# Retention attention feeding a gated MLP, one core: key casts of the first two units on ScalarE, and a new fixed order of all engines

## The chip, the cores and the metric

The kernel runs on one core of a Trainium2 chip. The metric is the device time of one execution in microseconds (us). The core has five instruction streams that run side by side and meet only at semaphores: TensorE (PE, with its weight loads PEld), VectorE (DVE), ScalarE (ACT), GpSimd (POOL) and SyncE (SP). SP issues the loads of q, k and v, the transposing DMAs and most stores; POOL issues the loads of the two weight matrices, since these convert fp32 to bf16 on the way.

## The reference

Attention without softmax over 8 batches, 8 heads, 576 positions and 64 columns, then an MLP with the gate h·cos(h):

```python
scores = q @ k.transpose(0, 1, 3, 2) / 8
ret = (scores * Dmat) @ v            # Dmat[h, i, j] = gamma_h ** (i - j) for i >= j, else 0
x = ret.transpose(0, 2, 1, 3).reshape(4608, 512)
h = x @ w_in                         # 512 x 2048
out = (h * cos(h)) @ w_out           # 2048 x 512
```

Inputs and output are fp32; the kernel multiplies in bf16.

## The kernel before

**Units and blocks.** The 576 positions of a batch are cut into two groups of 256 and a rest of 64. A *unit* (b, g) is group g of batch b, all heads. Two units, one from each batch of a pair, make a *block* of 512 rows for the MLP: block 0 is units (0,0) and (1,0), block 1 is (0,1) and (1,1), block 2 is (2,0) and (3,0), up to block 8, which holds the rests. A half of a block (256 columns of it) belongs to one unit.

**One unit** (`unit`, L585 to L632). SP loads k, q and v as fp32 tiles `stgk`, `stgq`, `stgv` of 512 KB. Each becomes a bf16 tile in two halves y = 0, 1: `natk` is a cast (L574 if ACT makes it, L575 if DVE or POOL does), `qnat` and `natv` are products with decay weights (L624). In the first four units (the blocks 0 and 1) `natk` and `qnat` are then turned by PE (`tpe`, L648: four 128x128 transposes into one PSUM bank), and each bank is copied to `kt` or `qt` (again L574 on ACT, L575 on DVE). Later units are turned by DMA.

**Attention of a unit** (PE, L694). `ses/` multiplies keys and queries (in the first two units in two steps), and DVE multiplies the result with the mask into four halves of `pt` (L743). `ses=` adds key-value products to a running state, which ACT copies out (`sba`, `sbb`). `ses:` and `ses+` multiply `pt` and values, and queries and states; the result goes to a half of `xt`, by ACT (L574) and DVE (L575). `ses:` needs all four halves of `pt`.

**MLP.** `m1` (L908) is one 128-column piece f of the first product, four matmuls over one or both halves of a block, followed by the cosine on ACT (L917) and the gate on DVE (L920). From block 3 on the first product is done with seven instead of eight block products (L1037); the second product is always done so (L1177, steps P1 to P7).

**Weights.** `load_w` on POOL (L888, L892) loads w_in and w_out in four slabs each. Slab s of w_in holds the pieces f = 4s to 4s+3. The issue of a slab is itself a POOL instruction, and waits for a gate: in `SLABS`, slab 0 waits for the load of q of unit (0,0), slab 2 for q of (1,0), slabs 1 and 3 for k of (1,0). The loads of unit (0,1) wait for slab 2 (`NEXT = 2`), the slabs of w_out for k of (1,1), the loads of (2,0) for slab 2 of w_out.

**The order.** Every piece of work is a task of a graph. `ORDER` is a string with two characters per task that give its rank; each engine takes its tasks strictly in that order (`lay`, `run`). `run` also counts through planned times (a task's `dur`, a load's `dma` and `tail`, `SHARES` for two kinds of loads at once, `FETCH` for the refill of PE's instructions). From these it chooses which buffer of a pool a task gets, where PE is given filler matmuls (`warm`, L517) in a planned gap, and some order between DVE and POOL. The planned times are nowhere else in the program.

Of the kernel before, what the change touches and what calls it, by code (L numbers as in the profile page):

```python
# [130 lines left out]
class Graph:  # L131


    BACKLOG, FIRST = 4000, 6000
    SHARES = (0.65, 0.30)
    FETCH = (3200, 1500, 2550, 2000)
# [116 lines left out]
    def run(self):  # L253
# [46 lines left out]
        while len(order) < len(self.tasks):  # L300
# [71 lines left out]
class Kernel:  # L372
# [18 lines left out]
        "#[#O#X$(#m$&#W#J#T#{#h#|#\\#T#\\$*#n$)#Y#M#Y$&#k$(#|#g#x$,#p$+#X#K#U#y#f#z#a#U#`#z#j$##c#X#f#w#c#t#i#]#g$)"
        "#o$*#Z#b#V#a#q#e#o#n#`#d#Y#q#t#r#k#p#e#g#h#\\$#$%$$#n#u#v#8$-$0#w#O#2#D#B#5#I#C#3#E#H#<$5$7$7$9$8$3$6#z$?"
        "$$$#$@$%#|#4#9#F#K#7#J#N#=#;#M#L#C#:#>#O#R#A#Q#T#?#@#S#P#F$>$B$?$<$A$@$F$,$+$G$'$&$\\$?$Z$O$0$I$[$>$V$_$C"
        "$[$S$6$Q$U$7$P$K$*$D$Z$=$U$J$($G$M$-$J$L$1$L$R$5$N$Q$3$K$Y$<$T$X$:$R$T$@$Y$2$4$,$6$5$;$>$=$4$8#x$2$:$:$;"
        "$<#y$9$=#{$A$D$B$C$E$C#`$H$I$)#P$N$H$F$.$/$P$2$4$V$;$9$W$8$S#B#G#W#Z#E#X#V#D#M#Y#`#Q#J#N#^#a#H#c#[#I#L#\\"
        "#d#V$]$X$W$B$A$b$D$G$c$E$^$o$l$k$M$R${$Y$Z$|$W$s#S#K#f#l#R#e#j#U#X#g#o#[#T#\\#i#t#Y#w#x#W#Z#k#q#g%'$w$x$^"
        "$a%.$l$m%/$f$|#U$E#]$M#_$d#b$n$`$b$e$f$`$F$k$J$f$K$i$n$N$r$p$b#p$p$m$Q#h$y$V$t$s$O$t$P$x$U$r$v$S$z$u$[#n"
        "$w$q$X#m%($_$y%%$\\%&$]%*$e%#%)$`%-${$j#s%+$z$d#r%1$k%(%,$c%3$i%2$h%%%0$g%4%&$n#v%6%'$p#u%9$q%.$]$_$\\$a$c"
        "$o$O$g$d$e$H$^$a$h$h$i$I$g$j$L$l$m$j%#%$$v#o$q$u$T#f%)%+%1%/%=$r%>$s%@$v%5%A$t%D%8%%$(%B%4%,$*%L%$%?%E$y"
        "%G$|%M%#%>%H${%K%<%($&%N%=%.$)%P%&%A%S%*%U%-%Y%1%G%V%2%]%H%7$,%Z%F%<$.%d%=%P%[%3%_%6%`%9%L%^%5%c%K%>$1%e"  # L400
        "%N%E$2%g%?%Q%$%*%0%2%:%6%9%7%5%7$o%:%?%3%<%F$z%;%C$w%O%T%B%I%J%;$&%X%\\%4#q%8%-%,$u$x%Q%)%'%R%+%@#d#]#{#y"
        "#a$$#z#^#e$##|#i#b#k$%$0#h$3$-#_#c$'$+#v%W%D%C%/%0%a%8%:%b%;%J%M%S%V%T%k%B%m%D%o%G%[%n%C%q%Y%H$8%r%Z%K$<"
        "%u%M%b%z%N%{%O&'%S%e&$%P&(%d%W$?&%%c%Z$A&-%Y%i&&%R&)%U&*%T%f&,%V&3%j%`$C&.%h%c$D&6%e%q&/%X&1%]&2%\\%k&4%^"
        "&9%p%h$F&7%n%d$E&>%i%v%E%I%U%X%^%]%W%\\%f%i%A%p%x%`%l%t%L%j%s%I&#&+%g%y%|%a$?&0&5%_$=%h%O%R%@%F%v%Q%[%w%J"
        "%_#l#m$7$/#n$:$5#p#j$4$6#|#s#t$9$=#w$@$B#r#u$;$>$+&8%o%m%b%a&<%f%l&=%g%r%s%u%{%x&@%j&E%o&C%n%|&D%m&I&%%x"
# [5 lines left out]
        "$*$($M$T$3$.$<$/$]$Z$;'1&[&T&Z&U'<&S&_&U&`&b&c&e&d'?&W'A&Y'B&\\&i'E&^'K&n&j$e'D&k&g$d'O&c&q'F&]'H&_'P&d&t"
        "'I&`'N&p&e$c'L&r&k$f'U&i&x'M&b'T&h'Q&o'#'W&l'[&w&p$g'Y''&y$i'^&r&{'Z&n'a&t'`&s'$']&q'b&|&u$h'f'+&z$j'e&v"
        "'&&a&l&j&m&g&v&s&o'@'G&a'S'V&u'R'X&m'C'J&f'\\'c'%'_'d'($A'i'j'#$C&y&z')','*'/'-'0'g'h&w&x'o'p'.$E$B'k'n&{"
        "&|'l'm'$'q'r'1'2$F$D's't'3'%'&'v'u'5'4$H$G"
# [6 lines left out]
    BOTH = ((0, 1),)  # L421
# [929 lines left out]
```

## Time and profile before

| | us |
|---|---|
| median of 3 runs (lowest, highest) | 282.84 (282.12, 283.46) |
| the profiled execution, its own time | 284.13 |
| its span, first to last instruction | 282.4 |
| PE busy | 270.7 |
| DVE, ACT, POOL busy | 227.3, 177.5, 161.2 |

The profiled execution is one execution: its span stands for work on the engines, its own time has what lies around that too, and the profiler adds a little; it is 1.29 us above the median. A busy PE in the profile is not a PE at its peak, since matmuls overlap: a 256-column matmul is shown as 273 ns, but the next one can start about 109 ns later. Lines with `[... <-X]` give the idle time of an engine before a row, and what ended it.

### The profile page before, as it was taken

The numbers are of one execution on the slowest core, as the hardware profiler recorded it, in microseconds if no ns is written. First come the engines' busy times: TensorE is split into PE (matmuls) and PEld (weight loads), VectorE is DVE, ScalarE is ACT, GpSimd is POOL, SyncE is SP. The second block draws the span as 40 slices with busy tenths as digits, with TensorE's granted clock in tenths as the row PEclk, the third lists the DMA queues.
The fourth block names the chain that finished last, engine by engine and source line by source line (L and its number), as shares of the span: only waits on it lengthen the run. The fifth ranks groups of instructions, "written<-read, shape, count | busy, mean of one in ns | idle before, by whom it ended". The sixth has DMA issues, their size and how long they took to land.

```text
span 282.4 us, 9745 instructions
## 1 busy us (share of the span) xinstructions
PE 270.7 (96%) x4136; PEld 219.9 (78%) x4136; DVE 227.3 (80%) x394; ACT 177.5 (63%) x367; POOL 161.2 (57%) x180
## 2 busy tenths in 40 slices
PE   6779989999999999979999999999999999999995
PEld 2457568888885468868888888888888888888884
DVE  3666889988974998868997996688759899997764
ACT  4346767255247765669469875885778865778530
POOL 4640872167377683897568757981375667216330
DMA  7999999999999999999999997979816090410016
GB/s 199 249 192 262 273 171 163 300 243 263 179 187 245 204 264 206 181 221 176 251 192 208 279 238 134 168 194 175 194 32 123 6 163 2 159 69 0 2 74 224
DMA packets 122731, 49.91 MB, mean 177 GB/s; under 512 B 84800, under 2 KB 118592, under 8 KB 122688
## 3 DMA queue, kind: packets, MB, share of 16 engines
q1 hardware_dynamic: 118176, 44.84, 74.8%
q0 software_dynamic: 4224, 4.19, 9.6%
q8 instruction: 32, 0.52, 0.8%
q10 hardware_dynamic: 288, 0.26, 0.3%
q14 instruction: 11, 0.09, 0.1%
HBM read 36.70 MB, written 9.44 MB: 163 GB/s over the span
## 4 chain that ended last, share of the span: by engine, by line
PE 84%; DMA 8%; POOL 3%; issue 2%; SPq 1%; DVE 1%; ACT 1%; DVEq 0%; ACTq 0%
PE bk L1177 38%; PE bk L1037 26%; PE bk L908 11%; PE bk L694 8%; DMA stgq<-in_q_dram 3%; DMA win<-in_moe_w_in_dram 3%; DMA stgk<-in_k_dram 3%; POOL natv L624 1%; SPq L585 1%; POOL qnat L624 1%; POOL gt L1026 1%; POOL win L888 0%; ACT xt L574 0%; DVE sq L1020 0%; PE bk L648 0%
## 5 line engine op out<-in xcount | busy, mean ns | idle before, releaser
L1026 POOL TENSOR_TENSOR gt<-sq,cb 128x512 bf16<-128x512 f32 x48 | 55.8, 1172 | 49.1 <-ACT cb L1022 27.0
L908 PE MATMUL bk<-xt,win 128*128 128x256 bf16 (+1 forms) x288 | 46.3, 308 | 1.8 <-DMA win<-in_moe_w_in_dram 0.9
L624 POOL TENSOR_TENSOR natv<-stgv,wv 128x512 bf16<-128x512 f32 x36 | 37.5, 1046 | 12.5 <-DVE s L1108 4.8
L920 DVE TENSOR_TENSOR gt<-bk,cb 128x256 bf16<-128x256 f32 (+1 forms) x72 | 34.5, 507 | 12.0 <-ACT cb L917 9.3
L917 ACT ACTIVATE cb<-bk 128x256 bf16<-128x256 f32 (+1 forms) x72 | 31.2, 455 | 19.6 <-PE bk L908 16.5
L624 POOL TENSOR_TENSOR qnat<-stgq,wq 128x512 bf16<-128x512 f32 x32 | 33.5, 1052 | 16.7 <-DVE s L1114 5.6
L1037 PE MATMUL bk<-xt,win 128*128 128x256 bf16 x288 | 41.0, 273 | 0.0
L1020 DVE TENSOR_TENSOR sq<-bk,sq 128x512 f32<-128x512 f32 x48 | 32.5, 684 | 8.9 <-PE bk L1037 5.0
L908 PEld LDWEIGHTS bk<-xt,win 128*128 128x128 bf16 x288 | 26.8, 98 | 15.3 <-DVE pt L743 1.2
L743 DVE TENSOR_TENSOR pt<-bk,tr 128x512 bf16<-128x512 f32 x48 | 31.1, 682 | 8.4 <-PE bk L694 8.1
L575 POOL CAST natk<-stgk 128x512 bf16<-128x512 f32 x34 | 20.7, 614 | 28.2 <-DMA stgk<-in_k_dram 15.7
L1177 PE MATMUL bk<-wout,gt 128*128 128x256 bf16 x288 | 36.7, 273 | 0.0
L1026 DVE TENSOR_TENSOR gt<-bk,cb 128x512 bf16<-128x512 f32 x48 | 32.3, 682 | 4.0 <-ACT cb L1022 3.8
L1177 PE MATMUL bk<-wout,s 128*128 128x256 bf16 x288 | 35.6, 273 | 0.0
L1177 PE MATMUL bk<-tw,s 128*128 128x256 bf16 x288 | 35.4, 273 | 0.0
L574 ACT ACTIVATE sq<-bk 128x512 f32<-128x512 f32 x48 | 27.7, 595 | 10.0 <-PE bk L1037 8.8
L1022 ACT ACTIVATE cb<-sq 128x512 bf16<-128x512 f32 x48 | 30.0, 632 | 5.4 <-DVE sq L1020 2.9
L1022 ACT ACTIVATE cb<-bk 128x512 bf16<-128x512 f32 x48 | 28.4, 598 | 6.7 <-PE bk L1037 3.7
L1177 PEld LDWEIGHTS bk<-tw,s 128*128 128x128 bf16 x288 | 28.0, 98 | 3.6 <-DVE pt L743 0.3
L1037 PEld LDWEIGHTS bk<-xt,win 128*128 128x128 bf16 x288 | 27.9, 98 | 3.6
L1177 PEld LDWEIGHTS bk<-wout,gt 128*128 128x128 bf16 x288 | 27.6, 98 | 3.7 <-issue 0.2
L1177 PEld LDWEIGHTS bk<-wout,s 128*128 128x128 bf16 x288 | 27.7, 98 | 3.5
(80 smaller groups left out, 436.5 us busy)
## 6 DMA issues: line engine op xcount, KB each, us to landing
stgq<-in_q_dram SPq DMA_DIRECT2D x16, 512.0 KB, 6.1
out_dram<-os SPq DMA_DIRECT2D x16, 512.0 KB, 4.4
stgk<-in_k_dram SPq DMA_DIRECT2D x20, 256.0 KB, 5.6
stgv<-in_v_dram SPq DMA_DIRECT2D x20, 256.0 KB, 5.4
stgk<-in_k_dram SPq DMA_DIRECT2D x6, 512.0 KB, 6.9
stgv<-in_v_dram SPq DMA_DIRECT2D x6, 512.0 KB, 7.4
win<-in_moe_w_in_dram POOLq DMA_DIRECT2D x4, 512.0 KB, 8.0
wout<-in_moe_w_out_dram POOLq DMA_DIRECT2D x4, 512.0 KB, 7.5
```

What stands on the lines that cost most here:

```text
L574: return self.one(eng, dur, lambda e: e.activation(dst(), src(), AF.Copy), r=r, w=w, **kw)
L624: self.one(eng, 610 if eng == "dve" else 1030, lambda e, out=out, inp=inp, tab=tab, col=col, hs=hs: e.tensor_tensor(out(), inp(), ap(tab, ...
L694: return lambda e: e.matmul(out(), lhs(), rhs(), start=start, stop=True, skip_group_check=True)
L743: self.one("dve", 610, lambda e, r=r, b=b, pt=pt: e.tensor_tensor(ap(self.at(pt), 1024, 0, 128, 512 * r, [64 * ny * ny, 8 // ny // ny], [1 ...
L908: inst = e.matmul(ap(self.at(bk), 512, 0, 128, 0, [1, n]), ap(self.WIN, 4 * DFF, 0, 128, c * DFF + 128 * f, [1, 128]), ap(self.at(xt), 204 ...
L917: self.one("act", n - 15, lambda e: e.activation(ap(self.at(cb), TB, 0, 128, 0, [1, n]), ap(self.at(bk), 512, 0, 128, 0, [1, n]), AF.Sin, ...
L920: self.one("dve", 75 + n / 0.96, lambda e: e.tensor_tensor(ap(self.at(gt), NF * TB, 0, 128, f * TB + 256 * h0, [1, n]), ap(self.at(bk), 51 ...
L1020: self.one("dve", 610, lambda e: e.tensor_tensor(half(src), self.at(bank).ap(), half(src), ALU.add), r=[(bank,)], w=four(src))
L1022: self.one("act", 530 if name else 490, lambda e: e.activation(self.at(cb).ap(), ap(self.at(src), size, 0, 128, 0, [1, 512]), AF.Sin, bias ...
L1026: self.one(eng, 1120 if name else 610, lambda e: e.tensor_tensor(ap(self.at(gt), NF * TB, 0, 128, (8 * n + 2 * g) * TB + 256 * h, [TB, 2], ...
L1037: inst = e.matmul(ap(self.at(bank), 512, 0, 128, 256 * f, [1, 256]), l(c, f), rr(c), stop=True, skip_group_check=True, start=(first and f ...
L1177: inst = e.matmul(place(bank, tt), l(f, tt), rr(f), stop=True, skip_group_check=True, start=(first and f == 0 and tt < len(bank)))
```

## The change

Four things are edited.

1. **The key casts of the units (0,0) and (1,0)**, second half (y = 1), go from POOL to ACT. The first half was on ACT already.
2. **The copies of transposed tiles**, y = 1, are on DVE for the units listed in `BOTH` alone. Before they were so for (0,0), (1,0) and (0,1); now for (0,0) and (0,1). So the two copies of unit (1,0) go to ACT; those of unit (0,0) stay on DVE.
3. **`ORDER`** is a new string for all 1477 tasks. 370 of the 444 PE positions hold another task, and most positions of the other engines too.
4. **Planned times**: `SHARES`, `FETCH`, `dma` and `tail` of the slabs. A constant that nothing used goes.

```diff
-    BACKLOG, FIRST = 4000, 6000
-    SHARES = (0.65, 0.30)
-    FETCH = (3200, 1500, 2550, 2000)
+    BACKLOG = 4000
+    SHARES = (0.80, 0.35)
+    FETCH = (3200, 1500, 3550, 5550)
...
-                    usable[k] = max(a + self.FETCH[0], dma_free + self.FETCH[1]) + self.FETCH[2] + self.FETCH[3] * (a < 45000)
+                    usable[k] = max(a + self.FETCH[0], dma_free + self.FETCH[1]) + self.FETCH[2 + (a < 45000)]
...
     ORDER = (
...
-    BOTH = ((0, 1),)
+    BOTH = ((0, 0), (0, 1))
...
-                    eng = ("act", "pool")[y] if fast else self.CASTS.get(u, "pp pp pp")[y]
+                    eng = "act" if fast else self.CASTS.get(u, "pp pp pp")[y]
...
-                        self.tpe(nb, 512 * y, [(y,)], t[dst], (y,), ("act", "dve")[y] if fast or u in self.BOTH else "act")
+                        self.tpe(nb, 512 * y, [(y,)], t[dst], (y,), ("act", "dve")[y] if u in self.BOTH else "act")
...
-                 sem=f"{which}{s}", dma=2750 if which == "win" else 3000, tail=900, prio=prio)
+                 sem=f"{which}{s}", dma=3350 if which == "win" else 3450, tail=500, prio=prio)
```

Read out of the two strings, with each rank set beside its task, the first tasks of the engines are (00 is unit (0,0), and so on; 0 or 1 behind it is y):

```
POOL before: natk 00/1, natv 00/0, natk 10/1, natv 00/1, win 0, win 2, natv 10/0, natv 10/1, win 3, win 1, natk 01 x2
POOL after:  natv 00/0, natv 00/1, win 0, win 2, natv 10/0, natv 10/1, win 3, win 1, natk 01 x2
ACT before:  natk 00/0, qt 00/0, kt 00/0, natk 10/0, sba 00, qt 10/0, kt 10/0, xt 00
ACT after:   natk 00/0, natk 00/1, kt 00/0, qt 00/0, natk 10/0, natk 10/1, sba 00, kt 10/0, kt 10/1, qt 10/0, qt 10/1, sbb 00, xt 00
DVE before:  qnat 00 x2, qt 00/1, kt 00/1, pt 00 x3, qnat 10 x2, pt 00, kt 10/1, qt 10/1, xt 00, pt 10 x4
DVE after:   qnat 00 x2, qt 00/1, kt 00/1, pt 00 x4, qnat 10 x2, xt 00, pt 10 x4
PE before:   tpe 00 x4, ses/ 00, tpe k 10/1, ses/ 00, tpe k 10/0, ses= 00, tpe q 10 x2, ses: ses+ 00, ses/ 10, ses= 10, ses/ 10, m1 f1 f3 f0 f2, ses: ses+ 10
PE after:    tpe 00 x4, ses/ 00, ses/ 00, tpe k 10/0, ses= 00, tpe k 10/1, ses: ses+ 00, tpe q 10 x2, ses/ 10, ses/ 10, m1 f0, ses= 10, m1 f2 f3 f1, ses: ses+ 10
```

The SP order is the same for the loads of the units (0,0), (1,0) and (0,1). Further on, PE's last step before block 1 (`ses+` of (0,1)) is followed at once by `m1` of block 1, where before one `m1` of block 0 and one `tpe` stood between; the first two slabs of w_out are issued before any half of unit (1,1) is made on POOL, the last two after its keys and queries; and `ses:` of unit (6,0) comes four tasks behind its `ses/`, where before thirteen stood between.

More of the change, by code (lines that the diff above doesn't have):

```diff
@@ L391 @@
[L391 to L405, printed above, removed]
@@ L411 @@
[L411 to L414, printed above, removed]
+        "###$###$#&###%#$###$#%#%#&#&#%###$#'#(#)#*#(#'#*#)#,#.#-#/#-#'#,#+#.#,#/#-#&#'#(#)#*#+#+#(#'#(#0#1#1#0#/"
@@ new lines @@
+        "#.#3#2#7#I#8#4#5#%#&#*#)#+#,#G#D#F#D#*#-#.#J#E#L#F#+#0#/#)#N#Q#I#J#L#M#P#K#T#]#U#N#N#,#8#5#b#[#`#Y#.#6#7"
+        "#Z#S#]#V#-#4#3#2#0#3#R#J#P#6#5#6#M#H#K#4#1#2#;#8#9#5#3#4#@#<#=#K#F#G#B#?#@#<#=#>#=#9#:#:#7#8#C#@#?#9#6#7"
+        "#?#;#;#O#L#O#H#C#E#I#G#H#E#B#C#D#A#B#A#>#A#>#:#<#S#M#Q#1#2#9#:#/#;#<#0#>#=#2#C#E#6#h#j#c#d#g#j#i#b#r#r#s"
+        "#f#e#V#e$'#t#b#i#q#n#\\#U#X#y#j#v$+#t$($,#v$*#V#O#R$5#{$2#f#`#a$)#s$&#c#\\#^$'#q$%#p#c#s$-#w$+#W#P#S$0#z$1"
+        "#[#T#W#z#k#|#X#Q#T#|#p$##_#X#Z$*#u$)#Y#R#U$&#o#{$##l#x#v#g#r#a#Z#\\#{#m#y#^#W#Y#w#h#u#e#^#_$%#n#z#d#_#`$."
@@ new lines @@
+        "#x$,#[#f#]#h#p#l#o#m#g#k#a#n#o#k#q#u#i#l#m#d$$$($$#t#x#w#<$/$4#|#L#1#?#@#4#B#A#5#F#D#8$1$3$-$.$0$/$2#y$8"
+        "$$$($9$'$##7#3#H#G#:#I#J#>#;#L#P#@#9#A#K#R#?#O#M#=#B#N#T#F$7$;$;$3$7$=$D$,$+$E$-$*$\\$D$V$]$F$Y$a$K$Z$[$B"
+        "$U$Z$E$W$Y$@$R$M$3$F$V$>$O$N$5$G$L$4$E$U$=$M$Q$7$J$P$8$K$O$6$H$W$?$P$T$;$Q$4$6$5$9$8$:$<$?$:$<$%$6$=$>$?"
+        "$@$&$>$A$)$B$C$@$F$J$A#z$G$H$.#Q$I$C$B$/$0$K$1$2$R$<$9$S$:$L#E#G#U#X#C#S#W#D#N#V#_#K#I#M#[#d#H#Z#Y#J#O#\\"
+        "#a#W$X$S$T$C$A$^$G$J$_$H$X$o$k$h$R$U$|$_$]%#$^$s#P#R#c#h#S#i#b#T#U#e#g#Z#X#\\#l#t#Y#w#u#V#[#k#o#g%'$u$v$e"
@@ L415 @@
+        "'I&c'L&j&n$c'N&l&x$g'P&i&n'R&k'V&m'U&p&u'W&o'[&w&w$e'Y&t&s$d'`&z'$'Z&q'_&v']&t&y'^&u'c&{&y$f'd'%'#$h'f'$"
+        "''&W&Y&i&q&o&p&x&v'?'B&^'K'S&r'T'\\&r'H'Q&l'a'b&|'X'k',$C'g'j'%$A&z'#'(')'-'&'+'*'e'h&|&{'m'o'.$E$B'l'n''"
+        "'&'i'p'('q'r'0'/$D$F's't'1')'*'v'u'3'2$H$G"
     )
```

25 lines of the change are left out of this document (15 added, 10 removed).

## Prediction

> **What bounds the kernel now.** First the page: the busy times, and the chain of work, to see which engine ends last.
>
> ```profile
> PE 270.7 (96%) x4136; PEld 219.9 (78%) x4136; DVE 227.3 (80%) x394; ACT 177.5 (63%) x367; POOL 161.2 (57%) x180
> ...
> PE 84%; DMA 8%; POOL 3%; issue 2%; SPq 1%; DVE 1%; ACT 1%; DVEq 0%; ACTq 0%
> ```
>
> PE sets the end, so the question is where PE is not at work. The busy time of a long stretch (its us, then PE, PEld, DVE, ACT, POOL, clock, DMA share, GB/s) and the waits of PE between 45 and 258 us (total, times, longest) answer for the middle:
>
> ```profile
> 126.00:258.00 132.00, 131.68 (x2082) 115.03 (x2080) 113.26 (x180) 98.76 (x196) 80.28 (x81) 1.00 0.73 150
> ```
>
> ```profile
> PE bk L694 <- issue: 1.7, 2, 1.5
> ```
>
> PE is full there but for two waits of 1.7 us in all. The work on PE is the same after the change, so the time can move only by (a) how early PE gets its work in the first 40 us, and (b) waits that the new order takes away from the middle or puts into it. For (a), the chain in order of time (start, us):
>
> ```profile
> 3.21 7.18 DMA stgk<-in_k_dram
> 10.45 0.61 POOL natk L575
> 11.06 1.00 POOL natv L624
> 12.06 0.89 POOL win L888
> 12.95 8.27 DMA win<-in_moe_w_in_dram
> 21.70 8.43 DMA stgq<-in_q_dram
> 30.21 1.76 POOL qnat L624 x2
> ...
> 38.69 0.76 ACT xt L574
> 39.57 3.22 PE bk L908 x28
> ```
>
> The start is a chain of loads: the keys of (1,0) land, POOL casts a half of them, makes a half of the values, and only then issues the w_in slabs; the loads of unit (0,1) follow the slabs; POOL turns them into tiles. At 39.57 block 1 begins and PE is full from there. Of PE's own rows in the head three matter, with their waits:
>
> ```profile
> 17.71 1.47 PE L908 MATMUL bk<-xt,win 128*128 128x256 bf16 x12 [0.88 <-DMA win<-in_moe_w_in_dram]
> ...
> 20.40 0.50 PE L908 MATMUL bk<-xt,win 128*128 128x256 bf16 x3 [0.68 <-issue]
> ...
> 38.22 0.22 PE L694 MATMUL bk<-natv,natk 64*64 64x64 bf16 x3 [0.71 <-issue]
> ```
>
> **The change, part by part.** *Key casts from POOL to ACT.* The second half of the first unit's cast was off the path (v lands later); that of (1,0) is the 10.45 row of the chain. POOL's other rows, and ACT's:
>
> ```profile
> 8.73 1.04 POOL L624 TENSOR_TENSOR natv<-stgv,wv 128x512 bf16<-128x512 f32 x1 [1.29 <-ACT qt L574]
> ...
> 13.94 2.04 POOL L624 TENSOR_TENSOR natv<-stgv,wv 128x512 bf16<-128x512 f32 x2 [0.23 <-DMA stgv<-in_v_dram]
> 15.93 1.55 POOL L888 DMA_DIRECT2D win<-in_moe_w_in_dram  x2
> ```
>
> ```profile
> 10.41 0.63 ACT L574 ACTIVATE natk<-stgk 128x512 bf16<-128x512 f32 x1 [1.19 <-DMA stgk<-in_k_dram]
> 12.60 0.38 ACT L574 ACTIVATE sba<-bk 128x256 bf16<-128x256 f32 x1 [1.55 <-PE bk L694]
> 14.29 0.60 ACT L574 ACTIVATE qt<-bk 128x512 bf16<-128x512 bf16 x1 [1.31 <-PE bk L648]
> 14.78 0.59 ACT L574 ACTIVATE kt<-bk 128x512 bf16<-128x512 bf16 x1
> 15.61 0.75 ACT L574 ACTIVATE xt<-bk 128x512 bf16<-128x512 f32 x1 [0.24 <-PE bk L694]
> ```
>
> POOL's first value half can't start before 8.73 (ACT is named there, but nothing of ACT is among its inputs; it is the load of v). The two halves then end at 8.73 + 2 × 1.04 = 10.8, and slab 0 is issued at 10.8 instead of 12.06: 1.2 us earlier. Slab 2 waits for q of (1,0), which is there by about 12.3 (k landed at 10.4, v at 13.9, by the rows at 10.41 and 13.94, and q lies between them), instead of 12.95. Slabs 3 and 1 stay at 15.93, behind the values of (1,0), and that costs nothing as long as slabs 0 and 2 are still moving. Does the earlier issue help? The engines' traffic by microsecond:
>
> ```profile
> 13.00:14.00 1.00, 0.45 (x5) 0.15 (x4) 1.00 (x3) 0.00 (x0) 0.77 (x2) 1.00 0.77 46
> 14.00:15.00 1.00, 1.00 (x44) 0.85 (x44) 1.00 (x3) 0.71 (x2) 1.00 (x2) 1.00 0.71 91
> 15.00:16.00 1.00, 1.00 (x49) 0.76 (x39) 0.45 (x2) 0.76 (x2) 1.00 (x2) 1.00 1.22 204
> ```
>
> After the last load of the two units the engines move data at 46 and 91 GB/s for two microseconds (last column), against 204 then: there is a hole of some 1.3 to 2 us in which only slab 0 starts up. An issue 1.2 us earlier fills it, so I take the full 1.2 us for every slab (bounds 0.65, slab 2's gain, and 1.25). By the 17.71 row slab 0 then lands at 16.5.
>
> [...]
>
> ```profile
> q0 software_dynamic: 560, 0.56, 124.1%
> ```
>
> That is the list of queues that moved a packet from 21.3 to 24.0: the slabs' alone, though the queries of (0,1) were issued at 21.70 (chain): a later request stands behind the earlier ones. So the loads of (0,1) follow the end of the slabs, 1.2 us earlier, and with them k, q, v on POOL (30.21 becomes 29.0).
>
> *ACT's own path.* ACT gets two casts (0.63 each) and two copies (0.59; DVE's take 0.41, row below) more. By its new list: casts of (1,0) 10.41 to 11.67; `sba` to 12.4; two `kt` copies to 13.55; the two `qt` copies wait for queries. DVE now does all four mask products first (0.65 apart, from 9.75 to 12.5) and then `qnat` of (1,0) to 13.85; PE turns it by 14.3; `qt` 14.3 to 15.5, `sbb` 15.9, `xt` 16.65 instead of 15.61 + 0.75 = 16.36. So `ses:` of (0,0) has its mask products at 12.5, which is worth nothing: `xt` ends 0.3 later on ACT than before, and the first `m1` starts at about 16.75 instead of 17.71, a gain of 1.0, bounded by ACT rather than the slab.
>
> ```profile
> 9.75 1.29 DVE L743 TENSOR_TENSOR pt<-bk,tr 128x512 bf16<-128x512 f32 x2 [0.63 <-PE bk L694]
> ...
> 14.32 0.41 DVE L575 COPY kt<-bk 128x512 bf16<-128x512 bf16 x1
> ```
>
> *From there to block 1.* PE has 32 half-pieces of `m1` of block 0, 0.44 us each (28 matmuls in the 3.22 of the 39.57 row are 7 halves), ahead of or between the attention of (0,1). POOL ends the queries of (0,1) at 30.21 + 1.76 = 31.97 now, at 30.8 after; being turned, copied and multiplied they reach the scores at about 32.3. PE's list is there at about 31.7 (20.4 less 1.2, 1.5 of `m1` and `ses:` of (1,0), some 25 half-pieces' worth of listed work), so data decides. Behind the scores the list is half an `m1` longer than before, and the wait of 38.22 is reached in the same step; if its packet comes as much earlier as the loads ahead of it, `ses+` ends 1.2 to 1.3 earlier, at about 37.4 (before, just ahead of the `xt` of 38.69). Then a loss: nothing stands any more between `ses+` and `m1` of block 1, so PE waits the whole 0.9 us for `xt` (38.69 to 39.57), where 0.24 of a `tpe` and 0.44 of an `m1` filled it. Block 1 begins at 38.3; before, without the `tpe`, it would be 39.57 - 0.24 = 39.33. **Head: -1.0 us** (bounds -0.3, if ACT or the wait at 20.40 takes the rest, and -1.4).
>
> *The waits called issue.* What ends them is no engine and no load:
>
> ```profile
> 125.45 0.25 PE L694 MATMUL bk<-natv,natk 64*64 64x64 bf16 x7 [1.46 <-issue]
> ```
>
> ```profile
> 117.50:124.00 6.50, 6.49 (x160) 5.41 (x157) 4.64 (x8) 5.79 (x14) 6.32 (x8) 1.00 1.05 233
> ```
>
> ```profile
> q8 instruction: 32, 0.52, 0.8%
> ```
>
> The instruction queue moves 32 packets of 16 KB; PE has 4136 matmuls and as many weight loads (first fence), 2 × 4136 / 32 = 258 per packet. I read the waits as PE reaching the end of its instructions before the next packet is there: between 38.22 and 125.45 lie 11 such packets and one wait, just where attention's small matmuls are densest (317 instructions in the 6.5 us before it). The new order keeps this place: the same steps stand there, so the 1.46 stays. It makes one new place of the same density, unit (6,0), whose `ses/` and `ses:` now lie in one such stretch (four tasks between them instead of thirteen), at about 6.2 us for 322 instructions by the same durations, and a milder one at (2,0) and (3,0), 7.8 us. The price of each is between 0 and 1.46. The one such wait arose with both stores and loads on the move; I take **+0.2** for both, near the low end, since 317 in 6.5 us is the only case of its kind and no wait stands at the next densest. What is left is +1.46 twice.
>
> [...]
>
> *Planned times, buffers.* These change nothing on the chip but buffer choice and filler matmuls. Fillers stand in planned gaps and cost nothing there, a few tenths where a gap is gone. I take 0. The new middle order is otherwise a reshuffle of work on which PE now waits 1.7 us in 213; I take 0, bounds -0.3 (the second wait gone) and +0.5.
>
> **Sum.** -1.0 + 0.2 = -0.8 us against the profiled execution, that is an own time of 283.3 instead of 284.13; against the median 282.84 - 0.8 = **282.0 us**, a little faster.
>
> **The rivals.**
>
> 1. *The packets shift, and the wait at 125.45 shrinks.* Where the blocks of 256 end depends on the number of fillers; ten more would move the dense place across a boundary and take about 0.6 to 1.46 off. For: the gaps of the head do change. Against: nothing says which way. With head -1.0 to -1.4: 282.84 - 2.2 = 280.6.
> 2. *ScalarE becomes the bound of the head.* Its list up to `xt` ends at 16.65 by the sum, 0.15 behind the slab; a slip of 1 us in `qnat` or the turned queries and `m1` starts where it did. For: it is serial, all on one engine. Against: 1.3 us of waits for queries lie in it. Gain zero, refill +0.2: 283.0.
> 3. *The refill waits decide, slower.* If a packet takes over 6.2 us from request to use at (6,0), and over 7.8 at (2,0), both new places cost the full 1.46. For: the head's two waits show packets that came late while loads were queued, and loads are queued at both places. Against: only one such wait in the 218 us from 40 to 258. -1.0 + 2.92 = +1.9: 284.7. It decides from a refill time of 6.2 us on; above it, each 0.1 us of it costs 0.1 per place.
>
> **How the numbers follow.** A measurement of this kernel can tell about 0.5% from no change, that is 1.41 us: below 281.43 is faster, above 284.25 slower. Forecast 0.45 (281.2 to 282.7 with its bounds; 0.13 of it below 281.43), rival 1 0.25 (all faster), rival 2 0.10 (all within), rival 3 0.20 (0.18 of it slower). Faster 0.13 + 0.25 = 0.38, slower 0.18, within 0.44. The range reaches from the far end of rival 1 (282.84 - 1.4 - 1.46 = 280.0) to rival 3's 284.7, 280.0 to 284.8.
>
> **What would show it.** Right: slab 0 issued near 10.8, no hole between loads and slabs, first `m1` near 16.7, `m1` of block 1 near 38.3, one wait of about 1.5 near 124. Wrong: first `m1` at 17.7 with ACT named (rival 2); waits called issue near 70 or 160 (rival 3); none near 124 (rival 1). If a wait on DVE or POOL shows in the middle, the reshuffle did what I took as 0.

## The result: slower by 1.1%, with a wide spread of executions

| | median | all executions |
|---|---|---|
| kernel before | 283.15 us | 282.84, 283.46, 282.12, 283.5 |
| changed kernel | 286.51 us | 285.74, 287.43, 285.0, 287.28 |

The ratio is 1.0109 (95% interval 1.0066 to 1.0152): slower by more than 0.5%, above the range of 280.0 to 284.8. The profiled execution of the changed kernel took 285.74 us by its own time (before: 284.13), its span is 284.0 us (before: 282.4). Ratios here leave out executions more than 1.5% above a kernel's fastest as disturbed; in the changed kernel those are executions with the lowered clock found below, so medians over all executions stand beside the ratios.

The page of the changed kernel, busy times and chain of work:

```profile
PE 274.7 (97%) x4140; PEld 221.5 (78%) x4140; DVE 223.3 (79%) x392; ACT 179.1 (63%) x371; POOL 160.4 (56%) x178
...
PE 88%; DVE 4%; POOL 3%; issue 2%; DMA 1%; ACT 1%; POOLq 0%; DVEq 0%; ACTq 0%
```

PE has the same matmuls (four fillers more) and is busy 4.0 us longer. Four fillers are some 1.3 us of it (24 of them are busy for 8.0 us before); a wait is not busy time, so PE is also slower somewhere. The stretch and the list of PE's waits that the prediction read in the middle say how much:

```profile
126.00:258.00 132.00, 129.59 (x2043) 112.26 (x2044) 109.07 (x174) 94.30 (x187) 80.33 (x80) 0.99 0.68 150
```

```profile
PE bk L694 <- issue: 2.1, 1, 2.1
```

The wait of 1.46 us at unit (5,0) is gone, and one of 2.1 us is new. PE's rows around it (start, us, then the matmuls and in brackets the wait ahead of them):

```profile
163.14 0.28 PE L694 MATMUL bk<-natv,natk 64*64 64x64 bf16 x11
165.54 0.24 PE L694 MATMUL bk<-natv,natk 64*64 64x64 bf16 x5 [2.12 <-issue]
...
166.75 1.84 PE L1177 MATMUL bk<-tw,s 128*128 128x256 bf16 x8
168.39 1.06 PE L1037 MATMUL bk<-xt,win 128*128 128x256 bf16 x4
```

This is `ses:` of unit (6,0) (in later units this step also carries key-value products, the rows `natv,natk`), the place of the prediction's third rival: PE stops at 163.23 in the middle of a step, at instructions whose packet ends at 164.12 us (the count is in the last section), for 2.3 us from start to start. The price has a second part that no row of before had shown. Behind the wait eight matmuls of L1177 take 1.84 us and four of L1037 1.06. The windows tell why (the number ahead of the last two is the granted clock):

```profile
162.00:166.00 4.00, 1.89 (x82) 1.47 (x80) 1.59 (x4) 1.32 (x4) 2.97 (x4) 1.00 1.49 280
166.00:170.00 4.00, 4.00 (x24) 2.81 (x23) 2.44 (x4) 1.41 (x3) 1.86 (x2) 0.60 1.11 81
170.00:174.00 4.00, 4.00 (x38) 3.49 (x37) 2.86 (x4) 3.56 (x7) 1.11 (x1) 0.97 0.91 223
```

For 4 us the clock is 0.60, which costs 4 × 0.40 + 4 × 0.03 = 1.7 us; with its ends set to 166.83 and 170.24 us the view gives 0.50. Wait and clock make 4.0 us.

The head, where the gain should be, in the rows that answer to those of before: POOL, then PE.

```profile
8.65 2.05 POOL L624 TENSOR_TENSOR natv<-stgv,wv 128x512 bf16<-128x512 f32 x2 [5.00 <-DMA stgv<-in_v_dram]
10.64 0.96 POOL L888 DMA_DIRECT2D win<-in_moe_w_in_dram  x1
12.43 0.75 POOL L888 DMA_DIRECT2D win<-in_moe_w_in_dram  x1 [0.83 <-DMA stgq<-in_q_dram]
13.90 2.04 POOL L624 TENSOR_TENSOR natv<-stgv,wv 128x512 bf16<-128x512 f32 x2 [0.72 <-DMA stgv<-in_v_dram]
15.89 1.55 POOL L888 DMA_DIRECT2D win<-in_moe_w_in_dram  x2
```

```profile
17.02 0.60 PE L908 MATMUL bk<-xt,win 128*128 128x256 bf16 x4
...
39.24 1.91 PE L908 MATMUL bk<-xt,win 128*128 128x256 bf16 x16 [0.39 <-ACT xt L574]
```

The issues are where the prediction put them (slab 0 at 10.64, slab 2 at 12.43, 3 and 1 at 15.89), the first `m1` starts 0.7 us earlier (17.02 for 17.71), but block 1 only at 39.24; 38.3 was forecast, and 39.33 is the like point of before. The engines' traffic shows where it went: the hole at 13 to 15 us is filled, and another has opened.

```profile
13.00:14.00 1.00, 1.00 (x56) 0.88 (x56) 0.99 (x2) 0.19 (x1) 0.28 (x2) 1.00 1.14 187
14.00:15.00 1.00, 1.00 (x12) 0.56 (x10) 0.74 (x1) 0.52 (x2) 1.00 (x2) 1.00 1.24 203
...
16.00:17.00 1.00, 1.00 (x23) 0.32 (x12) 0.69 (x2) 0.47 (x1) 1.00 (x2) 1.00 0.77 105
```

105 GB/s between 16 and 17: slab 0 is through near 16.8 (it lands 6.2 us after its issue by the list of DMA issues), and slab 2's data, issued at 12.43, can hardly move yet.

So the account of the two profiled executions is: head -0.1 to -0.3, the wait of (5,0) -1.5, a second small wait of before (the list there counts two) -0.2, the new wait at (6,0) +2.3, the clock behind it +1.7. That makes +2.0 to +2.2 against a span that grew by 1.6.

### The profile page after: what moved, and what is told of

Read it like the earlier page. It is cut to its first block, busy times and chain, and to the rows that moved or that the text cites. A ratio compares the mean times of both kernels' runs of the same rounds, so it can differ in the third digit from the quotient of the medians.

```text
span 284.0 us, 9768 instructions
## 1 busy us (share of the span) xinstructions
PE 274.7 (97%) x4140; PEld 221.5 (78%) x4140; DVE 223.3 (79%) x392; ACT 179.1 (63%) x371; POOL 160.4 (56%) x178
## 4 chain that ended last, share of the span: by engine, by line
PE 88%; DVE 4%; POOL 3%; issue 2%; DMA 1%; ACT 1%; POOLq 0%; DVEq 0%; ACTq 0%
PE bk L1177 38%; PE bk L1037 24%; PE bk L908 14%; PE bk L694 9%; DVE pt L743 2%; PE bk L648 2%; DMA stgq<-in_q_dram 1%; POOL gt L1026 1%; PE bk L517 1%; POOL qnat L624 1%; POOL natk L575 1%; DVE s L1114 0%; ACT qt L574 0%; DVE gt L920 0%; ACT xt L574 0%
## 5 line engine op out<-in xcount | busy, mean ns | idle before, releaser
L1026 POOL TENSOR_TENSOR gt<-sq,cb 128x512 bf16<-128x512 f32 x48 | 55.1, 1160 | 35.6 <-ACT cb L1022 17.7
L1037 PE MATMUL bk<-xt,win 128*128 128x256 bf16 x288 | 42.5, 275 | 0.1
L920 DVE TENSOR_TENSOR gt<-bk,cb 128x256 bf16<-128x256 f32 (+1 forms) x72 | 33.3, 507 | 7.9 <-ACT cb L917 6.3
L575 POOL CAST natk<-stgk 128x512 bf16<-128x512 f32 x32 | 19.7, 627 | 32.7 <-PE bk L908 10.7
L1177 PE MATMUL bk<-tw,s 128*128 128x256 bf16 x288 | 36.9, 277 | 0.0
L1177 PE MATMUL bk<-wout,gt 128*128 128x256 bf16 x288 | 36.4, 273 | 0.0
L1177 PE MATMUL bk<-wout,s 128*128 128x256 bf16 x288 | 35.7, 273 | 0.0
L574 ACT ACTIVATE sn<-bk 128x512 f32<-128x512 f32 (+1 forms) x29 | 16.1, 566 | 24.7 <-PE bk L1177 21.0
L1177 PEld LDWEIGHTS bk<-tw,s 128*128 128x128 bf16 x288 | 28.5, 99 | 3.8 <-ACT xt L574 0.2
L1037 PEld LDWEIGHTS bk<-xt,win 128*128 128x128 bf16 x288 | 27.5, 98 | 4.3 <-ACT sq L574 0.4
L1177 PEld LDWEIGHTS bk<-wout,gt 128*128 128x128 bf16 x288 | 27.9, 98 | 3.7
```

The lines of the kernel that those rows point to most:

```text
L574: return self.one(eng, dur, lambda e: e.activation(dst(), src(), AF.Copy), r=r, w=w, **kw)
L920: self.one("dve", 75 + n / 0.96, lambda e: e.tensor_tensor(ap(self.at(gt), NF * TB, 0, 128, f * TB + 256 * h0, [1, n]), ap(self.at(bk), 51 ...
L1026: self.one(eng, 1120 if name else 610, lambda e: e.tensor_tensor(ap(self.at(gt), NF * TB, 0, 128, (8 * n + 2 * g) * TB + 256 * h, [TB, 2], ...
L1037: inst = e.matmul(ap(self.at(bank), 512, 0, 128, 256 * f, [1, 256]), l(c, f), rr(c), stop=True, skip_group_check=True, start=(first and f ...
L1177: inst = e.matmul(place(bank, tt), l(f, tt), rr(f), stop=True, skip_group_check=True, start=(first and f == 0 and tt < len(bank)))
```

## The experiments

Theory W: the loss is the wait at (6,0) with the lowered clock behind it, and the head's gain is lost in the slab queue. Rivals: the copies and casts on ScalarE (E), or a loss that the new order spreads over the whole run (R). The tables give each kernel's median and its extremes over all executions, beside the kernel before on the same chip, and how many executions had a mean clock under 0.996 in the records. The diffs of this section are shortened, and where lines stand in brackets or begin with an engine or a step they tell the edit in words.

**1. The changed kernel again** (no edit).

> The changed kernel once more, unaltered. Theory W (the loss is a new instruction wait of TensorE in unit (6,0) near 163 us, about 2.2 us, and a lowered granted clock behind it, about 1.6 us, against one wait of 1.46 us that is gone): 285 to 287 us, 2.0 to 3.5 us over the kernel before, and in this profile again an issue wait over 1.5 us on a line L694 between 160 and 168 us with a granted clock under 0.8 in the next 4 us. Rival R (the new order loses a little everywhere, and that wait was chance): the same time, but without that wait or at another place.

| | median (lowest, highest) | before on the same chip | mean clock under 0.996 |
|---|---|---|---|
| changed kernel | 284.62 (280.75, 288.03) | 283.44 (282.4, 286.75) | 5 of 11 |

The ratio is 0.9994 (0.9962 to 1.0027). The same program takes 280.75 or 288.03 us. The five with the lower clock took 285.5 to 288.03, the six others 280.75 to 284.62, with a median of 283.17 (283.34 for the kernel before on this chip, without its two of lowered clock). W's forecast failed in both halves: the median lies under its 285 to 287, and the profiled execution is the one of 280.75 us and has no wait called issue in the middle. By itself that is what R foretold, a wait by chance. But it makes the best comparison there is, one program twice. Its rows at (6,0) and the window behind:

```profile
162.35 0.32 PE L694 MATMUL bk<-natv,natk 64*64 64x64 bf16 x16
...
163.73 1.05 PE L1177 MATMUL bk<-tw,s 128*128 128x256 bf16 x8
```

```profile
166.00:170.00 4.00, 4.00 (x39) 3.52 (x38) 3.51 (x5) 3.89 (x8) 2.56 (x3) 1.00 0.98 159
```

```profile
38.16 1.91 PE L908 MATMUL bk<-xt,win 128*128 128x256 bf16 x16 [0.38 <-ACT xt L574]
```

All sixteen matmuls of the step run through, the eight of L1177 take 1.05 us for 1.84, the clock is 1.00, and block 1 starts at 38.16, 1.08 us earlier than in the first profile. Of the 1.08 us, 0.8 are left at (6,0) (163.14 for 162.35). Behind wait and clock the same matmuls lie 4.7 us apart (170.72 and 175.41 us): 0.8 + 2.3 + 1.6. The last 0.5 of the 5.2 us between the two spans (284.0 and 278.8) arise between 212 and 221 us, and no row tells why. So W's wait and clock are 3.9 us of this difference, the largest part; the head's gain is there in one execution and not in the other. They are not all of the spread: without a lowered clock the six still differ by 3.9 us, and of the first four executions two at a clock of 1.00 took 285.0 and 287.28 us, the latter with 3.2 us outside its span for 1.7 to 1.8 in the others.

**2. All block boundaries 32 instructions earlier.**

```diff
-            for _ in range(n):      # first call: 9 matmuls of 512 columns
+            for _ in range(n + 16): # first call: 25 matmuls of 184
```

> The changed kernel with the first nine filler matmuls cut into 25 narrower ones of the same total width: 32 more TensorE instructions, so that every block boundary falls 32 instructions earlier in the work, and no other order or engine changed. Counted on the order, the stretch between request and need at (6,0) grows from about 6.5 us to over 7.6 us. Theory W: no wait at (6,0) and no lowered clock behind it, 3 to 4 us less than the changed kernel, 282.0 to 283.0 us, unless the stretch at (5,0), which shrinks from 6.4 to 5.8 us, waits in its place for up to 1.5 us (then 283.5 to 284.5). Rival R: within 0.7 us of the changed kernel.

Measured 283.72 us (282.42 to 284.72), ratio 1.0006 (0.9984 to 1.0027), lowered clock in 1 of 12. The wait at (6,0) is gone and with it everything above 285; the rival's "within 0.7" of 284.62 fails by a little (0.9), W's "3 to 4 less" holds against the executions with the lowered clock, not against the median, and its 282.0 to 283.0 is missed. The one wait in its profile that is called issue is 1.0 us long, near 72.6 us and not at (5,0): moving the boundaries trades one place for another.

**3. Slab 2 issued directly behind slab 0.**

```diff
-    SLABS = ((0, 'q', 0, 100), (2, 'q', 1, 101), ...
+    SLABS = ((0, 'q', 0, 100), (2, 'k', 1, 101), ...
```

> The changed kernel with slab 2's issue gated on the key load of (1,0), which lands at 10.3 us, in place of the query load (12.1): the issue moves from 12.4 to about 11.7 us, directly behind slab 0's, as far from it as in the kernel before. Theory H (head: slab 2's data come 4.6 us after its issue in the changed kernel, with the queue nearly empty from 15.5 to 17.0, and this loses the gain of slab 0's early issue): the hole closes, slab 2 lands at 19.0 to 19.7 instead of 20.4, the loads of (0,1) about 1 us earlier, block 1 starts 0.5 to 1 us earlier and the time falls by 0.5 to 1.0 us if the waits further on stay as they are. Rival: the software queue can't go faster and slab 2 lands at 20.3 to 20.5 all the same; no change.

Measured 284.55 us (281.73 to 287.7), lowered clock in 5 of 12. In the profile the hole is closed (first column again the stretch, last the GB/s):

```profile
16.00:17.00 1.00, 1.00 (x22) 0.53 (x11) 0.77 (x2) 0.40 (x1) 1.00 (x3) 1.00 1.25 214
```

214 for 105. The landing of slabs 3 and 1, from the list of DMA issues (the last number is the median time from issue to landing of the two), first of the changed kernel, then of this one, issued at the same times within 0.2 us:

```profile
win<-in_moe_w_in_dram POOLq DMA_DIRECT2D x2, 512.0 KB, 8.8
```

```profile
win<-in_moe_w_in_dram POOLq DMA_DIRECT2D x2, 512.0 KB, 8.0
```

0.8 us sooner, as H said; but block 1 starts at 39.10 for 39.24, not 0.5 to 1 us earlier, the time is that of the changed kernel within its spread, and in this profiled execution (286.77 us) (6,0) waits again, 2.5 us by the list of waits, with a clock of 0.57 behind it. In kernel 1, with slab 2's issue where the change has it, the same list says 7.6. So the gate is not what decides.

**4. The engine moves alone, in the old order.**

```diff
-    (natk y = 1 of the units (0,0), (1,0): POOL;  qt, kt y = 1 of (1,0): DVE)
+    (the same four on ACT; order, slots, 24 fillers of the kernel before)
```

> The kernel before with only the engine moves of the change (key casts of (0,0) and (1,0) and both copies of the transposed tiles of (1,0) on ScalarE), its order of the work, its 24 fillers and its planned times left as they were. Theory W: the moves themselves cost or gain little: slab 0 is issued 0.6 to 1.2 us earlier, the rest of the head waits for data, 282.2 to 283.3 us, within 0.6 us of the kernel before, and the wait of 1.5 us near 125 us stays. Rival E (the copies on ScalarE are the loss): 1.5 us or more slower than the kernel before, with TensorE waiting for ScalarE's copies between 12 and 20 us.

Measured 283.88 us (282.74 to 286.06), ratio 1.0018 (0.9995 to 1.0042): 0.44 us over the median of before, within the 0.6, though above the 283.3 that W had as the upper end. By the median E falls: 1.5 us are not there. ACT ends `xt` of (0,0) at 17.08 (16.31 + 0.77), 0.7 us later than before, so the first `m1` gains nothing from a slab that was issued at 10.76. By the median the moves alone cost a little or nothing. The profile shows that this is a balance. The wait near 125 us, which was to stay, is 0.35 us by its row, and block 1 starts 1.5 us later than before (41.07 for 39.57):

```profile
41.07 1.14 PE L910 MATMUL bk<-xt,win 128*128 128x256 bf16 x9 [0.16 <-ACT xt L576]
```

What is late there are loads, not ScalarE: slabs 3 and 1 take 10.2 us from the issue for 9.0, and POOL has the queries of (0,1) at 31.66 for 30.21.

**5. The cut: 32 instructions more just ahead of (6,0).** The sharpest test of W, since it touches no order and no engine.

```diff
-                        for tt in (q,) if halves else range(2):
-                            inst = e.matmul(place(bank, tt), l(f, tt), rr(f), ...
+                        for tt, x in [(tt, x) for tt in range(2) for x in range(2)]:  # block 3, P4 only
+                            inst = e.matmul(128 columns of place(bank, tt), l(f, tt), the same 128 of rr(f), ...
```

> The changed kernel with the 16 matmuls of one product (P4 of block 3, two steps near 152 and 154 us) cut into two halves of 128 columns each: 32 more TensorE instructions just ahead of unit (6,0), everything before and every order as it was. The request of the block that (6,0) needs falls about 1.6 us earlier against the loads of (7,1), and the stretch until it is needed grows from 6.6 to 8.1 us by the count. Theory W (half of the executions of the changed kernel wait 2.2 to 2.7 us at (6,0) and then run 4 us at a granted clock of 0.60): no execution with a mean clock under 0.997, none above 284.8 us, median 282 to 283.3, at least 1.2 us under the changed kernel's. Rival R (the spread of 280.8 to 288.0 us has its cause in the head or outside the span): the same spread and as many executions with the lowered clock.

> The changed kernel with P4 of block 3 cut into halves, the kernel that ran at a median of 282.36 us, once more beside the next three. Theory W (without the wait at (6,0) the changed kernel stands a little under the kernel before): 282.0 to 282.8 us, no execution with a mean clock under 0.992 and none above 285. If 282.36 was luck of that chip or day: a median of 283.5 or more.

| | median (lowest, highest) | before on the same chip | mean clock under 0.996 |
|---|---|---|---|
| first run | 282.36 (281.23, 284.41) | 283.09 (282.2, 285.34) | 1 of 12 |
| second run | 283.14 (280.74, 285.19) | 283.48 (282.23, 288.1) | 0 of 12 |

Ratios 0.9977 (0.9954 to 1.0001) and 0.9965 (0.9928 to 1.0002). W holds: sixteen matmuls cut in two, 0.4% more instructions, take the executions of 285.5 to 288 away. In the changed kernel and kernel 3, which keep the boundary where it was, 12 of 27 executions have the lowered clock; in the four runs with the cut (these and 9 and 10) 2 of 48. The kernel before has it too, in 8 of the 92 executions that stand beside these runs, though in neither of its two profiles. The first run kept its bounds but for one execution of 283.09 us with a mean clock of 0.993. The second missed its upper bound of 282.8, and two executions at a clock of 0.999 (285.01 and 285.19) lie above its 285. Its profile has a wait called issue at another place, near 74 us, and none of the lowered clock. This is the prediction's milder new place, at (2,0) and (3,0), and up to there the program is the changed kernel's:

```profile
74.17 0.24 PE L694 MATMUL bk<-qt,sba 64*64 64x128 bf16 x2 [1.48 <-issue]
```

```profile
74.00:78.00 4.00, 3.83 (x80) 3.18 (x81) 2.46 (x6) 1.57 (x3) 1.05 (x1) 1.00 0.74 185
```

**6. Loads held back.** SyncE's first key load of (7,1) waits for a PE step.

```diff
+    after += [PE step P1 of block 4, second half]     # for the first key load of (7,1)
```

> The changed kernel with the first key load of (7,1), which SyncE issues at 158.55 us, and all of SyncE's queue behind it held until a TensorE step that ends near 159.8 us: the loads start 1.2 us later or more, no count and no order of TensorE changed. Theory Q (the block's packet comes 1.7 us after its request when the load queue is empty, at 157.4 in the execution of 280.75 us, and 5.3 to 5.6 us after it when the loads of (7,1) get ahead of it): the packet comes within 2.5 us of its request, lands more than 2 us before the boundary, no wait at (6,0), no execution with a mean clock under 0.997, median 282 to 283.5. If the delay of the packet has nothing to do with these loads: as many executions with a lowered clock as in the changed kernel (5 of 11), and the same median, 284.6.

The expectation had a fact wrong: 158.55 is the issue of the second half of these keys; the first went out at 153.4. Held were both, the first to 160.62. Measured 283.96 us (283.06 to 287.46), ratio 1.0026 (1.0003 to 1.0048), lowered clock in 0 of 12. The wait at (6,0) shrank to 0.15 us, but not for Q's reason. What moved on all queues from 157.0 to 161.5 us, and the packet of instructions then (the list of queues from 161.5 to 162):

```profile
DMA packets 0, 0.00 MB, mean 0 GB/s; under 512 B 0, under 2 KB 0, under 8 KB 0
```

```profile
q8 instruction: 1, 0.02, 17.3%
```

The packet comes only after 161.5, although for 4.5 us nothing moved that could stand ahead of it (when it was asked for, no profile shows; the times from a request in this and the other expectations are the author's estimates). Q falls, and its time with it: 282 to 283.5 was expected, and one execution took 287.46 us at a clock of 1.00. In the first profile of the changed kernel the packet also comes after 161.5 (161.88 to 164.12), in the execution of 280.75 us of kernel 1 between 157.0 and 158.5, alone on the queues:

```profile
q8 instruction: 1, 0.02, 28.1%
```

```profile
q8 instruction: 1, 0.02, 4.2%
```

PE needs it near 162.5 to 163.5. Early, it is there some 5 us ahead of need; late, PE stops, for 2.12 us in the first profile and for 0.15 us here. Why it comes early or late stays open.

**7. Waits of a known cause in the kernel before.** TensorE waits for a row of small copies on GpSimd, near 101 and near 189 us.

```diff
+    M1 of block 3 (PE) waits for 5 copies on POOL that wait for the PE step ahead of it
+    M2 of block 6 (PE) waits for 14 such copies
```

> The kernel before with two waits put into TensorE's queue: near 101 us TensorE waits for five small copies on GpSimd (estimate 0.8 to 1.2 us of wait), near 189 us for fourteen (estimate 2 to 3 us), both in stretches without a block boundary. Theory C (the lowered granted clock follows any TensorE wait of about 2 us, and doesn't follow one of 1.5 us): a granted clock of about 0.6 for some 4 us behind the wait at 189, worth about 1.6 us, and 1.0 behind the wait at 101; the time is 283.4 plus both waits plus 1.6. Rival: the clock stays at 1.0 behind both, and the lowered clock at (6,0) has a cause of its own there; the time is 283.4 plus both waits.

Measured 294.32 us (293.9 to 294.58), ratio 1.0386 (1.0344 to 1.0428). GpSimd had other work queued, so both waits came out longer than the estimates; the list of waits (sum, times, longest) and the windows that hold the 4 us after each:

```profile
PE bk L1049 <- POOL lg L518: 8.5, 2, 5.3
```

```profile
106.00:110.00 4.00, 3.94 (x94) 2.79 (x95) 0.00 (x1) 0.24 (x1) 1.55 (x2) 0.58 1.32 142
110.00:114.00 4.00, 4.00 (x38) 3.60 (x37) 4.00 (x8) 2.16 (x5) 0.00 (x0) 1.00 1.27 260
...
202.00:206.00 4.00, 4.00 (x26) 3.02 (x25) 1.20 (x2) 1.93 (x4) 0.00 (x0) 0.63 0.87 141
206.00:210.00 4.00, 4.00 (x82) 3.42 (x80) 3.13 (x7) 0.49 (x2) 0.00 (x0) 1.00 0.00 1
```

Behind 3.1 and 5.3 us of wait the clock is 0.58 and 0.63 in the window of 4 us, then 1.00 again; the windows ahead of these, 102 to 106 and 198 to 202 us, have 0.99 and 0.94, so the lowered clock costs 4 × (0.42 + 0.01) and 4 × (0.37 + 0.06), 1.7 us each time. Both waits end on copies of GpSimd and not on instructions, so the lowered clock belongs neither to (6,0) nor to the waits called issue alone. The sum agrees within 0.7 us: 283.09 + 8.5 + 1.7 + 1.7 = 295.0 for 294.32. That a wait of 1.5 us leaves the clock alone isn't shown by this kernel, whose shorter wait came out at 3.1; in the other profiles the clock is 1.00 behind 1.46 us (the kernel before), 1.48 us (above) and 0.90 us (next kernel).

**8. The kernel before again** (no edit).

> The kernel before once more, unaltered, for a second profile. Theory W: the wait of 1.5 us near 125 us at (5,0) is there or not by the time at which its packet comes (5.2 us after its request in the first profile); without it this execution is near 282 us by its own time, with it near 283.5.

283.77 us, near the 283.5 of a case with the wait. The wait at (5,0) is there, 0.90 us by its row, with the clock at 1.00 behind it:

```profile
125.17 0.25 PE L694 MATMUL bk<-natv,natk 64*64 64x64 bf16 x7 [0.90 <-issue]
```

```profile
126.00:130.00 4.00, 4.00 (x102) 3.41 (x101) 3.63 (x7) 4.00 (x9) 3.07 (x4) 1.00 1.09 139
```

**9. and 10. The head with the wait at (6,0) out of the way.** Both stand on kernel 5. One puts natv(1,0) behind the issues of slabs 3 and 1 on GpSimd, the other is kernel 3's gate.

```diff
-POOL: natv 00 x2, win 0, win 2, natv 10 x2, win 3, win 1
+POOL: natv 00 x2, win 0, win 2, win 3, win 1, natv 10 x2     # 9
```

> The same with GpSimd's two steps of natv(1,0), which ran at 13.9 to 15.9 us between the issues of slab 2 (12.4) and of slabs 3 and 1 (15.9 and 16.7), behind these issues: slabs 3 and 1 are issued at about 13.2 and 14.0, natv(1,0) runs at 14.8 to 16.9. Theory H2 (while GpSimd computes, the data of an issued slab don't get on: slab 2's come only when natv(1,0) is done, 4.6 us after their issue, and the hole of 15.5 to 17 us in the queue takes the gain of the early slab 0 away): no 1-us stretch from 14 to 22 us under 185 KB on the slab queue, slab 3 lands at 22.3 to 23.0, slab 1 at 25.3 to 26.0, the loads of (0,1) and block 1 up to 0.8 us earlier, 0.3 to 0.8 us less than without this. Rival: the hole stays at the same place, since it hangs on the time from the issue; then natv(1,0) is 0.9 us later for nothing, and the time the same or up to 0.5 us more.

> The same as the first with slab 2 gated on the key load of (1,0), so that it is issued at 11.7 us, 2.2 us ahead of natv(1,0), and that wait's place at (6,0) is out of the way this time. Theory H2: no hole at 15.5 to 17, slab 1 lands 0.3 to 0.8 us earlier than in the first, and the time is 0.2 to 0.7 us less: 281.7 to 282.4 us, the fastest of the kernels here. Rival: the head's end hangs on the total rate of both queues, and nothing is gained: within 0.2 us of the first.

| kernel | median (lowest, highest) | ratio to before (283.48) | block 1 starts in the profile |
|---|---|---|---|
| 5, second run | 283.14 (280.74, 285.19) | 0.9965 (0.9928 to 1.0002) | 40.53 |
| 9, natv behind | 282.70 (280.6, 284.32) | 0.9968 (0.9944 to 0.9991) | 38.54 |
| 10, gate on k | 283.09 (281.46, 284.86) | 0.9991 (0.9964 to 1.0018) | 38.75 |

Kernel 9's traffic and the start of block 1:

```profile
16.00:17.00 1.00, 1.00 (x35) 0.66 (x36) 0.39 (x1) 0.78 (x2) 0.85 (x1) 1.00 0.98 158
...
19.00:20.00 1.00, 1.00 (x8) 0.53 (x6) 0.91 (x4) 0.64 (x3) 0.00 (x0) 1.00 1.24 206
```

```profile
38.54 1.91 PE L908 MATMUL bk<-xt,win 128*128 128x256 bf16 x16 [0.40 <-ACT xt L574]
```

The hole at 16 to 17 stays (158), so H2's mechanism is not shown; from 17 us on the queue moves over 200 GB/s, block 1 starts at 38.54, and the median is 0.44 less than without. That is inside the spread of both, and kernel 5's own two profiles have block 1 at 39.42 and 40.53. Kernel 10 closes the hole (213 GB/s from 16 to 17, 156 in kernel 5's second profile), its slabs 3 and 1 take 8.3 us from the issue for 9.7, and it gains nothing that can be measured: its 281.7 to 282.4 is missed. Kernel 9 is the only one of these experiments whose interval lies wholly under 1 against the kernel before: 0.9968, about 0.9 us. One such interval among ten is a weak sign of a gain.

**11. The same cut in the kernel before**, ahead of (5,0) (product P7 of block 2).

> The kernel before with one product cut in the same way (P7 of block 2, near 109 to 111 us), so that the block boundary in unit (5,0) is asked for 1.6 us earlier; its wait there was 1.65 and 1.09 us in two profiles. Theory W: that wait goes, 281.8 to 282.6 us, which is what the changed kernel without its own wait has: the change's order then gains nothing by itself against the kernel before without a wait. If the change's order is worth something by itself: this kernel stays 0.5 us or more above the changed kernel with its cut.

Measured 284.43 us (282.96 to 285.21), ratio 1.0027 (1.0008 to 1.0047): slower, a miss. The long wait is 0.64 us in this profile, now in the unit's `ses/`; first the two rows ahead of the 125.17 row of kernel 8, then this kernel's:

```profile
123.76 0.45 PE L694 MATMUL bk<-qt,kt 64*64 64x64 bf16 x32
124.02 0.26 PE L694 MATMUL bk<-natv,natk 64*64 64x64 bf16 x9
```

```profile
123.83 0.39 PE L694 MATMUL bk<-qt,kt 64*64 64x64 bf16 x25
124.85 0.25 PE L694 MATMUL bk<-qt,kt 64*64 64x64 bf16 x7 [0.64 <-issue]
```

It is the same boundary, 7 + 9 = 16 matmuls or 32 instructions earlier, so the edit moved it as meant; but it still lies in (5,0), in a stretch as dense, and PE still stops there. Why the median rose by 0.95 us is not explained by that row. Against W's last sentence the changed kernel with its cut is 1.3 us under this one; so the change's order may be worth something by itself, but since the cut does not do the same in both kernels, the comparison doesn't settle it. Against the kernel before uncut (283.48) it is 0.3 us under.

## Why the prediction was wrong

- **"Head: -1.0 us" was half right.** The issues came where it had them. The step that failed is "I take the full 1.2 us for every slab", with "Slabs 3 and 1 stay at 15.93 ... and that costs nothing". The queue runs dry at 16 to 17 instead (105 GB/s), and in the first profile the two slabs took 8.8 us from the issue, for the 9.0 of before, so that they landed only 0.2 us earlier. In the execution of 280.75 us of the same program they took 7.6, and block 1 started at 38.16: the forecast 38.3 was met there. But six profiles have the change's head (kernels 1, 2, 5 twice, 6 and the first), and block 1 starts in them at 38.16 to 40.53, on average at 39.5. The four profiles with the head of before have it at 39.38 to 39.57, less 0.24 for the `tpe` 39.1 to 39.3. So the term of -1.0 came out between -1.2 and +1.2, and on average as no gain: block 1 starts at a time that differs by over 2 us from execution to execution, since the loads ahead of it do. In the latest of these profiles the engines move 160, 178 and 146 GB/s in the three microseconds from 19 us on, in the earliest 207, 201 and 207. Why is open: kernel 3 closed the hole at 16 to 17 us and had block 1 at 39.10 all the same. ScalarE's path was sized well (first `m1` at 17.02 and 16.65 in the two profiles of the unaltered program, forecast 16.75).
- **"What is left is +1.46 twice", and +0.2 for the new places: the term that was mis-sized.** The places were right. (2,0) and (3,0) have no wait of note in the two profiles of the unaltered program, but one of 1.48 us in the second of kernel 5, which is the same program up to there. The price at (6,0) was bounded by the one wait that the trace of before showed, 0 to 1.46 us. It came out as 0 or as 2.3 + 1.7 = 4.0 us, the latter in 7 of the 15 executions of the unaltered program, if the lowered clock marks them. A bound taken from a single row was no bound.
- **The lowered clock was missing from the list of prices.** No window of before that the prediction quotes has it in the middle: behind its wait of 1.46 us the clock is 1.00, as it is behind the 1.48 us in kernel 5's second profile.
- **"So the 1.46 stays" failed.** It is gone in both profiles of the changed kernel, and in before it was 1.46 and 0.90. Unit (5,0) stands where it stood; what differs is when the packet comes: it ends at 123.84 us in the kernel before, where PE goes on at 125.45, and at 120.30 in the first profile of the changed kernel, where PE runs through at 122.91. Rival 1's sign, no wait near 124, came true without its gain.
- **The rivals.** The third was the right mechanism with the wrong sum: 284.7 stood for two places at 1.46 each, and one place at 4.0 gave about the same. It lies between the medians 284.62 and 286.51. Rival 2 had the head's gain at zero, which is the average, but by ScalarE, and it was the loads. The forecast of 282.0 is within what the program does (280.75 to 288.03), and not its middle.
- How far 286.51 itself is explained: two of its four executions have the lowered clock; the other two, 285.0 and 287.28 us, have not, and no profile shows why they are slow. Over the second run's eleven the median is 1.2 us above the kernel before, not 3.4.
- The engine moves as such cost 0.4 us or nothing by the median (kernel 4).

## What to carry over

Where an engine with thousands of instructions is full, count its instructions per microsecond: in this kernel a stretch in which some 320 of them pass in 6 to 7 us (317 in the 6.5 us ahead of the wait of 1.46) is a place where it can run out, and whether it does can change from one execution to the next (2.12 us at (6,0) in one profile of the changed kernel, nothing in the other). So compare several executions and look at the clock of each before a reordering is judged by a median of four. A start that hangs on loads differs from one execution to the next in the same way (block 1 at 39.24 and 38.16 us in these two). A place of the first kind can be moved by a few instructions ahead of it (here sixteen matmuls cut in two), but only to where the next boundary is not dense as well.

## What the runs showed of the hardware

- A TensorE wait of 0.90, 1.02, 1.46 or 1.48 us left the granted clock at 1.00; with 2.1, 2.5, 3.1 and 5.3 us the window of 4 us behind shows 0.60, 0.57, 0.58 and 0.63. In the first profile of the changed kernel, with the ends set to 166.83 and 170.24 us, the view gives 0.50 over 3.41 us, which loses 1.7 us; this stretch begins 1.3 us behind the end of the wait of 2.1 us. The two stretches of kernel 7 lose 1.7 us each as well, but begin ahead of the end of the wait: the clock is 0.99 and 0.94 in the windows that end at 106 and 202 us, and PE goes on at 106.06 and 201.68.
- Length alone does not decide. Early in kernel 4 TensorE waits just as long, from 5.41 us on, and no lowered clock follows: the four transposes behind the wait take 0.40 us, as four do at 11.02 us in the first profile of the changed kernel, at a clock of 1.00. What decides beside the length, no run shows.

```profile
7.53 0.40 PE L650 MATMUL bk<-idn,natk 128*128 128x128 bf16 x4 [2.12 <-ACT natk L576]
```

- The waits called issue lie whole numbers of 256 instructions of PE apart, by a count of its matmuls, weight loads and semaphore instructions in the first profiles of the two kernels. In the kernel before 511 and 2817 start between the waits that end at 20.40, 38.22 and 125.45 us, 2 and 11 times 256 within one; 450 start ahead of the first of them, and 5314 ahead of the wait that ends at 165.54 us in the changed kernel, 19 times 256 more. The packets, 16 KB each, keep step: from wait to wait there are 2, 11 and 19 of them. Ahead of the four waits a packet ends at 18.98, 36.82, 123.84 and 164.12 us, and PE goes on 1.40 to 1.61 us later.
- The instruction packet can stay away while every DMA queue is idle (none moved from 157.0 to 161.5 us in kernel 6), so its lateness is not only a matter of other transfers, if it was asked for by then. Few of the packets cost anything (32 in each of the same two profiles, and at most two waits called issue between 45 and 258 us in any profile here), but one cost up to 4.0 us, with the lowered clock behind its wait.
- One program's executions spread over 7.3 us (280.75 to 288.03) with the wait in some of them, and over 3.2 to 4.5 us with the cut. In the profiles with the change's head the start of block 1 alone differs by 2.4 us (38.16 to 40.53).
